# Delta-rule attention with a two-level expert layer: values times norms made two chunks in advance, inverses spread a period behind their last step, selection products a period behind their factors

## The chip, the cores and the metric

The kernel is one program on one core of a Trainium2 chip. The metric is the device time of one launch in microseconds (us). The core's engines each run their own queue in the order in which the program was written: TensorE (PE) multiplies matrices, VectorE (DVE), ScalarE (ACT) and GpSimd (POOL) work elementwise, SyncE (SP) starts most of the transfers. An engine waits at an instruction until the results it needs are there, and everything behind that instruction in the same queue waits with it.

## The reference: what is computed

Two stages, one after the other. The first is a delta-rule attention over 4 batches x 8 heads, 768 steps, head size 48. The second routes each of the 3072 tokens to one of 4 groups, then to one of 4 experts in it, and applies that expert's two matrices.

```python
k_n = k / (norm(k) + 1e-6)
for t in range(S):                         # S = 768
    y[t]  = q[t] @ state
    v_old = k_n[t] @ state
    state = state + beta[t] * outer(k_n[t], v[t] - v_old)
x = y as (3072 tokens, 384)
g = argmax(x @ w_group); e = argmax(x @ w_expert[g])
out = softmax weight of g * softmax weight of e * (relu(x @ w1[g, e]) @ w2[g, e])
```

## The kernel before

**Chunks and periods.** The 768 steps are cut into `NCH` = 24 chunks of `C` = 32 steps; a chunk holds 4 batches x 32 steps = 128 tokens, so it fills the 128 partitions. One pass of the loop `for u in range(NCH + 1)` (line 612) is called a period here. Period u advances chunk u through the recurrence (`advance(u)`), and beside it works ahead and behind for other chunks. All work of the four engines in this part is written out by hand in one order (a `manual_schedule`); no scheduler moves it.

**The recurrence** (`advance`, four steps between its yields). L355 puts the scaled values `vh` into a PSUM tile `a_ps`, L361 adds keys times the old state `s_bd`; ScalarE copies it to `f` (L365); L370 makes the queries' part of the output in `o_ps`. L377 multiplies `f` by the chunk's inverse `mtb` to `w_ps`, ScalarE copies that to `w` (L380). L387 adds keys times `w` to the state in PSUM, ScalarE copies the state to `s_bd` (L393, two instructions). L398 finishes `o_ps`, ScalarE copies it to `x` (L402).

**The inverse.** Inside a chunk the 32 steps depend on each other; `inverse(g)` removes that with a 32 x 32 triangular inverse for each head, batch and chunk. It works on a group g of `RG` = 4 chunks at once, all on VectorE, in some 105 instructions: a transpose (L243), the norms (L250 to L280, the result `norm`), a scaling of `m` and a tile `cs` (L282, L287), elimination steps (L294, L299, L316, L322), a product with `cs` (L324), and a transpose to `mt` (L329). `mt` takes the buffer of `cs`, of which there is one. Then two ScalarE copies (L334) spread `mt` into the two halves of `mtb`. `gram(u)` makes what the inverse starts from, `LEAD` = 9 chunks ahead: L225 on TensorE, a ScalarE copy `gt` (L228) and a VectorE product `gq` (L233), both out of one PSUM tile of the tag "g".

**The routing.** `logits(u)` transposes `x` (L419, `t_ps`, also tag "g"), copies it (L423) and multiplies by the routing weights (L427, `l_ps`; L429 `lg`). `route(r)` takes the logits of 4 chunks (2 at the end), finds group and expert (VectorE, L454 to L482), counts tokens (POOL `acc` L484; TensorE L490 and L491 into `r_ps`, tag "g" again), and makes each token's place in its expert's list (`rk` L496, `place` L498) and its factors `mine` (L518). For each chunk it then makes a one-hot tile `at` on POOL (L523) and multiplies it with `mine` on TensorE (L529). These selection products collect the token lists in `s_sort`.

**Work that is due later.** `inverse` and `route` are generators. `start` puts one in the list `behind`; `work(n)` lets those with budget left run until each has used its share. A generator can yield a label instead of a number: it then stands still until `allow(label)` is called at a fixed point of the period. `SOON` is allowed near the end of a period, `NEXT` near its start, `SORT` and `ACT_STEP` after `w_ps`, `ACT_STEP` and `PE_STEP` also after the last step, `TURN` when a task ends. What is emitted at such a point stands at that place in the engine's queue, whether its input is ready by then or not.

**Buffers that matter here.** The PSUM tag "g" has one buffer, shared by the tiles of `gram`, `t_ps` and `r_ps`; so has tag "s", shared by `a_ps`, `w_ps` and `l_ps`. `vh`, `at`, `mtb` and `m` have two buffers, `mine` three.

**The second stage** walks the 16 experts in order of their load (a fixed list of row counts, `SLOTS`): gather rows (POOL L719), transpose (L729), two matrix products (L740, L754), transpose back (L766), scale and scatter (L769, L770).

Of the kernel before, what the change touches and what calls it, by code (L numbers as in the profile page):

```python
# [8 lines left out]
F32 = mybir.dt.float32  # L9
# [6 lines left out]
C = 32  # L16
RG = 4
# [4 lines left out]
ACT_STEP, PE_STEP, SOON, NEXT, TURN = "ScalarE", "TensorE", "end of the period", "next period", "its turn"  # L22
# [40 lines left out]
def deltanet_then_moe(  # L63
# [14 lines left out]
    B, H, S, D = shape  # L78
# [75 lines left out]
    with ExitStack() as first:  # L154
# [49 lines left out]
                pieces.pop(0)()  # L204

        rooted = sm.tile([128, 1], F32, tag="rooted", name="rooted", bufs=1)
        gts, gqs, mts, norm, vhs, xs = {}, {}, {}, {}, {}, {}

        def gram(u, home=None):

# [26 lines left out]
        def inverse(g):  # L237
# [43 lines left out]
            yield  # L281
            nc.vector.tensor_tensor(m, m, r0[:, :, None].to_broadcast([128, C, C]), op=ALU.mult)  # L282
            yield C * C
            while g and g - 1 not in mts:
                yield TURN
            cs = wk.tile([128, C, C], F32, tag="cs", name=f"cs{g}", bufs=1)
            nc.vector.tensor_tensor(cs, cut["below"].rearrange("p (i j) -> p i j", i=C),  # L287
# [37 lines left out]
            yield C * C  # L325
            nc.vector.tensor_scalar(diag, r0, -1.0, None, op0=ALU.mult)
            yield
            mt = wk.tile([128, RG * H, C], F32, tag="cs", name=f"mt{g}", bufs=1)
            nc.vector.transpose(out=mt.rearrange("p r i -> p i r"), in_=flat)  # L329
            mtb = wk.tile([128, RG * H, 2, C], F32, tag="mtb", name=f"mtb{g}")  # L330
            yield 2 * C * C
            for a in range(2):
                yield ACT_STEP
                nc.scalar.activation(mtb[:, :, a], mt, ACT.Copy,  # L334
                                     scale=cut["parity"][:, a:a + 1])
            mts[g] = mtb

        def scale(u):

            g, uu = divmod(u, RG)  # L340
            vh = wk.tile([128, H, D], F32, tag="vh", name=f"vh{u}")
            nc.vector.tensor_tensor(  # L342
                vh.rearrange("p (j f) d -> p f j d", f=2),
                kv_[u % NV][:, H * 64:].rearrange("p (j f d) -> p f j d", j=NP, f=2),
                norm[g][:, uu * H:(uu + 1) * H].rearrange("p (f j) -> p f j", f=2)[:, :, :, None]
                .to_broadcast([128, 2, NP, D]), op=ALU.mult)
            vhs[u] = vh
# [84 lines left out]
        def route(r):  # L432
# [53 lines left out]
            if n == RG:  # L486
# [31 lines left out]
            nc.vector.tensor_tensor(mine, hotf[:, :, None, :].to_broadcast(like),  # L518
                                    what[:, u0:u0 + n, :, None].to_broadcast(like), op=ALU.mult)
            yield 128  # L520
            for g, u in enumerate(us):
                at = wk.tile([128, T, TILE], F32, tag="at", name=f"at{u}")
                (nc.gpsimd if n == RG else nc.vector).tensor_scalar(  # L523
                    at.rearrange("p t i -> p (t i)"), cut["places"], place[:, u:u + 1], None,
                    op0=ALU.is_equal)

                yield SORT
                for t in range(T):
                    nc.tensor.matmul(s_sort[:, t * 3 * NE:(t + 1) * 3 * NE], lhsT=at[:, t],  # L529
                                     rhs=mine[:, g].rearrange("p c e -> p (c e)"),  # L530
                                     start=False, stop=True, skip_group_check=True)
# [19 lines left out]
        def work(n):  # L551


            for task in behind:
                due[task] = min(due[task] + n * 180 * rate[task], 4000.0)
            while True:
                able = [t for t in behind if held.get(t) is None and due[t] > 0]
                if not able:
                    break
                for task in able:  # L560
                    push(task)

        def allow(what):

            for task in list(behind):
                if held.get(task) is what:
                    push(task)
# [5 lines left out]
        with tc.manual_schedule(engines={mybir.EngineType.PE, mybir.EngineType.DVE,  # L573
                                         mybir.EngineType.Activation, mybir.EngineType.Pool}):
            nc.scalar.activation(rooted, cut["tiny"], ACT.Exp)
            homes = [None, s_ps[:, 0:2], s_ps[:, 2:4]]
            masks = []
            for u in range(RG):
                if u == len(homes):
                    masks.pop(0)()  # L580
                masks.append(gram(u, homes[u % len(homes)]))
                if u == 1:

                    nc.scalar.activation(kqt_[RG][:, 0, 0, 0:1], cut["tiny"], ACT.Copy)
                    load_rest()
            start(inverse(0), 1)
            for step in range(RG):
                work(6)
                masks.pop(0)()
                work(6)  # L590
                allow(ACT_STEP)
                allow(SOON)
                allow(NEXT)
                masks.append(gram(RG + step, homes[(RG + step) % len(homes)]))
            while behind:
                work(4)
                allow(ACT_STEP)
                allow(SOON)
                allow(NEXT)
                if masks:  # L600
                    masks.pop(0)()
            scale(0)
            nc.gpsimd.memset(acc[:, 0], 0.0)
            nc.gpsimd.tensor_copy(what[:, :, 0:2], cut["ids"].rearrange("p (u c) -> p u c", c=2))
            start(inverse(1), SHARE)
            for step in range(4):
                work(14)
                allow(ACT_STEP)
                allow(SOON)
                allow(NEXT)  # L610
                if step < LEAD - 2 * RG:
                    gram(2 * RG + step)()
            for u in range(NCH + 1):
                step = advance(u) if u < NCH else iter([None] * 4)
                turned = logits(u - 1) if u else iter([None] * 2)
                next(step)
                allow(NEXT)
                r = group_of.get(u - 2)
                if r is not None and group_of.get(u - 1) != r and r < NGR - 2:
                    start(route(r), 0.25)  # L620
                next(turned)
                if u + 1 < NCH:
                    scale(u + 1)
                work(16)
                next(step)
                allow(SORT)
                allow(ACT_STEP)
                masks = gram(u + LEAD) if u + LEAD < NCH else lambda: None
                work(9)
                masks()  # L630
                work(8)
                next(step)
                next(turned)
                next(step)
                allow(PE_STEP)
                allow(ACT_STEP)
                r = group_of.get(u - 1)
                if r is not None and group_of.get(u) != r and r >= NGR - 2:
                    start(route(r), 0.6 if r == NGR - 2 else 1)
                allow(SOON)  # L640
                if u % RG == RG - 2 and u // RG + 2 < NGR:
                    start(inverse(u // RG + 2), SHARE)
                work(12)
                if u + NB < NCH:
                    load_kq(u + NB)
                if u + NV < NCH:
                    load_kv(u + NV)
                if u < NCH:
                    nc.sync.dma_start(out=x_dram[u * 128:(u + 1) * 128], in_=xs[u])
                if pieces and u >= RG:  # L650
                    pieces.pop(0)()
            while behind:
                work(2)
                allow(PE_STEP)
                allow(ACT_STEP)
                allow(SOON)
                allow(NEXT)
                allow(SORT)

            n_ps = ps.tile([128, NE], F32, tag="s", name="n_ps")  # L660
            nc.tensor.matmul(n_ps, lhsT=ones, rhs=acc[:, NCH], start=True, stop=True)
            nc.vector.tensor_copy(found.rearrange("p t c e -> p (t c e)"), s_sort)
            by_place(found[:, :, :, 0:FIXED], slice(0, FIXED))
            nc.vector.tensor_copy(last, n_ps)


            key, rank = cp.tile([128, NE], F32, name="key"), cp.tile([128, NE], F32, name="rank")
            nc.vector.scalar_tensor_tensor(key, in0=last, scalar=16.0, in1=cut["tie"], op0=ALU.mult,
                                           op1=ALU.add)
            like = [128, NE, NE]  # L670
            nc.vector.tensor_tensor(table, key[:, None, :].to_broadcast(like),
                                    key[:, :, None].to_broadcast(like), op=ALU.is_gt)
            nc.vector.tensor_reduce(rank, table, axis=AX.X, op=ALU.add)
            nc.vector.tensor_tensor(table, rank[:, None, :].to_broadcast(like),
                                    cut["expert"][:, :, None].to_broadcast(like), op=ALU.is_equal)
# [241 lines left out]
```

## Time and profile before

Three launches took 583.02, 583.09 and 580.49 us, median 583.02. The profiled launch took 582.09 us, of which the profile shows a span of 580.3 us.

| engine | busy us | share of the span |
|---|---|---|
| TensorE matmuls | 502.1 | 87% |
| TensorE weight loads | 459.6 | 79% |
| VectorE | 251.8 | 43% |
| ScalarE | 164.4 | 28% |
| GpSimd | 105.0 | 18% |

The shares are averages over two stages with different limits: from about 288 us on the expert matrices keep TensorE busy without a break, and before that four engines hand work to each other. In the first stage the start of L355 marks the start of a period; the timeline of TensorE has it at these times.

| chunk u | L355 starts at, us | chunk u | L355 starts at, us | chunk u | L355 starts at, us |
|---|---|---|---|---|---|
| 0 | 49.42 | 8 | 130.29 | 16 | 207.31 |
| 1 | 61.85 | 9 | 139.39 | 17 | 216.37 |
| 2 | 71.98 | 10 | 147.77 | 18 | 224.04 |
| 3 | 82.66 | 11 | 157.49 | 19 | 231.71 |
| 4 | 92.66 | 12 | 168.97 | 20 | 239.39 |
| 5 | 100.54 | 13 | 179.11 | 21 | 247.06 |
| 6 | 108.50 | 14 | 187.49 | 22 | 254.89 |
| 7 | 116.79 | 15 | 196.04 | 23 | 262.78 |

Reading a line of the timeline: start in us, length in us, engine, line of the kernel, operation, output <- inputs, shape, number of instructions merged; in brackets how long the engine had been idle before it, and what it waited for. A line of the waits reads: who waited <- for whom: us in total, how often, the longest.

### The profile page before, as it was taken

The numbers are of one execution on the slowest core, as the hardware profiler recorded it, in microseconds if no ns is written. First come the engines' busy times: TensorE is split into PE (matmuls) and PEld (weight loads), VectorE is DVE, ScalarE is ACT, GpSimd is POOL, SyncE is SP. The second block draws the span as 40 slices with busy tenths as digits, with TensorE's granted clock in tenths as the row PEclk, the third lists the DMA queues.
The fourth block names the chain that finished last, engine by engine and source line by source line (L and its number), as shares of the span: only waits on it lengthen the run. The fifth ranks groups of instructions, "written<-read, shape, count | busy, mean of one in ns | idle before, by whom it ended". The sixth has DMA issues, their size and how long they took to land.

```text
span 580.3 us, 18417 instructions
## 1 busy us (share of the span) xinstructions
PE 502.1 (87%) x8166; PEld 459.6 (79%) x8166; DVE 251.8 (43%) x913; ACT 164.4 (28%) x324; POOL 105.0 (18%) x110
## 2 busy tenths in 40 slices
PE   3315779979989899997599999999999999999993
PEld 2214567867767778786599999999999999999993
DVE  1889989898898896123531111110111111111110
ACT  2103345544635545543011111111111111111110
POOL 0000000020021110130234221423225312221111
PEclk9999979989979979998599999999999999999998
DMA  8990334434422222210145747575766775676400
GB/s 280 404 382 12 112 104 152 144 110 136 129 85 81 62 82 89 73 56 31 49 142 155 223 158 224 177 228 178 239 202 192 236 226 204 241 239 216 160 20 18
DMA packets 44322, 90.64 MB, mean 156 GB/s; under 512 B 9756, under 2 KB 29651, under 8 KB 44241
## 3 DMA queue, kind: packets, MB, share of 16 engines
q1 hardware_dynamic: 34256, 79.71, 40.9%
q0 software_dynamic: 9984, 9.74, 6.3%
q8 instruction: 65, 1.06, 0.8%
q14 instruction: 17, 0.13, 0.1%
HBM read 79.92 MB, written 9.66 MB: 154 GB/s over the span
## 4 chain that ended last, share of the span: by engine, by line
issue 32%; PE 21%; DVE 19%; POOL 12%; DMA 9%; ACT 5%; POOLq 0%; SPq 0%; ACTq 0%; DVEq 0%
DMA out_dram<-yo,to_i 8%; POOL xg L719 7%; POOL out_dram L770 5%; DVE m L322 3%; DVE t L316 3%; PE s_ps L387 3%; PE w_ps L377 3%; PE a_ps L355 3%; ACT s_bd L393 3%; PE a_ps L361 2%; DVE m L299 2%; PE s_ps L529 2%; PE o_ps L370 2%; PE l_ps L427 1%; PE t_ps L419 1%
## 5 line engine op out<-in xcount | busy, mean ns | idle before, releaser
L740 PE MATMUL h_ps<-xt,w 128*128 128x224 f32 (+14 forms) x768 | 140.2, 336 | 0.6 <-DVE xt L731 0.6
L754 PE MATMUL y_ps<-hid,w 128*128 128x224 f32 (+14 forms) x768 | 138.8, 334 | 0.0
L740 PEld LDWEIGHTS h_ps<-xt,w 128*128 128x128 f32 x768 | 131.1, 192 | 1.6 <-DVE xt L731 0.9
L754 PEld LDWEIGHTS y_ps<-hid,w 128*128 128x128 f32 x768 | 129.3, 190 | 0.3
L731 DVE COPY xt<-t_ps 128x336 f32<-128x336 f32 (+14 forms) x32 | 15.1, 472 | 141.0 <-PE t_ps L729 141.0
L743 ACT ACTIVATE hid<-h_ps 128x448 f32<-128x448 f32 (+14 forms) x64 | 32.4, 506 | 125.7 <-PE h_ps L740 125.7
L769 DVE TENSOR_SCALAR yo<-o_ps,gate 112x384 f32<-112x384 f32 (+14 forms) x32 | 19.6, 616 | 106.3 <-PE o_ps L766 106.3
L719 POOL DMA_INDIRECT xg<-x_dram,from_i x32 | 39.3, 1227 | 121.5 <-PE t_ps L729 100.1
L770 POOL DMA_INDIRECT out_dram<-yo,to_i x32 | 39.2, 1226 | 101.8 <-DVE yo L769 100.9
L316 DVE TENSOR_TENSOR t<-m 128x81 f32<-128x81 f32 (+13 forms) x156 | 51.3, 329 | 0.2
L322 DVE TENSOR_TENSOR m<-m,t 128x81 f32<-128x81 f32 (+13 forms) x156 | 50.6, 324 | 0.0
L756 ACT ACTIVATE yt<-y_ps 128x224 f32<-128x224 f32 (+14 forms) x48 | 16.2, 338 | 120.2 <-PE y_ps L754 120.2
L355 PE MATMUL a_ps<-vh,con 128*128 128x384 f32 x48 | 26.2, 633 | 26.0 <-DVE vh L342 15.2
L393 ACT ACTIVATE s_bd<-s_ps 48x768 f32<-48x768 f32 x46 | 37.1, 806 | 22.2 <-PE s_ps L387 21.7
L299 DVE SCALAR_TENSOR_TENSOR m<-m 128x29 f32<-128x29 f32 (+27 forms) x174 | 39.2, 228 | 0.4
L523 POOL TENSOR_SCALAR at<-con,place 128x256 f32<-128x256 f32 x20 | 20.8, 1047 | 97.4 <-PE s_ps L529 49.7
L355 PEld LDWEIGHTS a_ps<-vh,con 128*128 128x128 f32 x48 | 8.4, 219 | 28.7 <-DVE vh L342 15.4
L377 PEld LDWEIGHTS w_ps<-f,mtb 64*64 64x64 f32 x768 | 25.3, 138 | 7.0 <-issue 4.9
L377 PE MATMUL w_ps<-f,mtb 64*64 64x48 f32 x768 | 28.5, 224 | 1.7 <-ACT f L365 1.0
L361 PEld LDWEIGHTS a_ps<-s_bd,kqt 128*32 128x32 f32 x736 | 17.0, 120 | 15.2 <-issue 15.2
L387 PE MATMUL s_ps<-w,kv 32*128 32x96 f32 x736 | 28.8, 296 | 0.2
L484 POOL TENSOR_TENSOR acc<-acc,hots 128x16 f32<-128x16 f32 x20 | 5.1, 256 | 129.2 <-DVE hots L482 128.0
(117 smaller groups left out, 551.6 us busy)
## 6 DMA issues: line engine op xcount, KB each, us to landing
w<-in_w_dram SPq DMA_DIRECT2D x28, 1536.0 KB, 7.5
kqt<-in_kq_dram SPq DMA_DIRECT2D x24, 512.0 KB, 5.1
kv<-in_kv_dram SPq DMA_DIRECT2D x24, 448.0 KB, 3.4
x_dram<-x SPq DMA_DIRECT2D x24, 192.0 KB, 2.3
w<-in_w_dram SPq DMA_DIRECT2D x6, 512.0 KB, 9.7
w<-in_w_dram SPq DMA_DIRECT2D x4, 576.0 KB, 10.1
w<-in_w_dram SPq DMA_DIRECT2D x2, 384.0 KB, 9.6
con<-in_const_dram SPq DMA_DIRECT2D x1, 512.0 KB, 8.2
```

Of the source, the lines that this page charges most:

```text
L299: nc.vector.scalar_tensor_tensor(row, in0=m[:, j, 0:j], scalar=m[:, i, j:j + 1], in1=row, op0=ALU.mult, op1=ALU.add)
L316: nc.vector.tensor_tensor(tv, m[:, j + 2:, j:j + 1].to_broadcast([128, n, j]), m[:, j:j + 1, 0:j].to_broadcast([128, n, j]), op=ALU.mult)
L322: nc.vector.tensor_tensor(below, below, tv, op=ALU.add)
L355: nc.tensor.matmul(a_ps.rearrange("p h d -> p (h d)"), lhsT=ident, rhs=vh.rearrange("p h d -> p (h d)"), start=True, stop=(u == 0), skip_g ...
L377: nc.tensor.matmul(w_ps[b, h], lhsT=mt[b, uu * H + (h % 2) * NP + h // 2], rhs=f[b, h], start=True, stop=True, skip_group_check=True)
L387: nc.tensor.matmul(s_at[:, b, j], lhsT=k[quads[b], j], rhs=w[quads[b], 2 * j:2 * j + 2], start=(u == 0 and j == 0), stop=True, skip_group_ ...
L393: nc.scalar.activation(s_bd[rows, :, :, hh, :], s_at[rows, :, :, hh * D:(hh + 1) * D], ACT.Copy)
L719: nc.gpsimd.indirect_dma_start(out=xg[0:P, t, :], out_offset=None, in_=x_dram[:, :], in_offset=bass.IndirectOffsetOnAxis(ap=rows[0:P, t:t ...
L740: nc.tensor.matmul(h_ps[:, k], lhsT=w1[:, j, (f + k) * 128:(f + k + 1) * 128], rhs=xt[:, j], start=(j == 0), stop=(j == DC - 1), skip_grou ...
L743: nc.scalar.activation(hid[:, f:f + 2], h_ps, ACT.Relu)
L754: nc.tensor.matmul(y_ps, lhsT=w2[:, f, j * 128:(j + 1) * 128], rhs=hid[:, f], start=(f == 0), stop=(f == FC - 1))
L770: put = nc.gpsimd.indirect_dma_start(out=out[:, :], out_offset=bass.IndirectOffsetOnAxis(ap=to[0:P, i:i + 1], axis=0), in_=yo[:, :], in_of ...
```

## The change

The order of three kinds of work is moved; no arithmetic is added or removed.

1. `scale(u)`, the product of values and norms `vh`, is made two chunks ahead instead of one: the first two before the loop, and `scale(u + 2)` near the end of period u in place of `scale(u + 1)` in its middle.
2. After the transpose L329 the inverse of every group but the first waits for the start of the next period before it spreads `mt` over `mtb` on ScalarE. Since `mt` then lives longer, it gets a buffer of its own, and the next group's `cs` waits for the transpose (`turned_over`) instead of for `mtb`; `TURN` is allowed once in every period.
3. In `route`, for the groups of four chunks, the one-hot tiles `at` and with them the selection products L529 wait for the end of the period after `mine`, so the first product stands a period later in TensorE's queue.

The purpose is that the engine which uses a result finds it ready when its turn comes.

```diff
-        gts, gqs, mts, norm, vhs, xs = {}, {}, {}, {}, {}, {}
+        gts, gqs, mts, norm, vhs, xs, turned_over = {}, {}, {}, {}, {}, {}, set()
...
-            while g and g - 1 not in mts:
+            while g and g - 1 not in turned_over:
                 yield TURN
             cs = wk.tile([128, C, C], F32, tag="cs", name=f"cs{g}", bufs=1)
...
-            mt = wk.tile([128, RG * H, C], F32, tag="cs", name=f"mt{g}", bufs=1)
+            mt = wk.tile([128, RG * H, C], F32, tag="mt", name=f"mt{g}", bufs=1)
             nc.vector.transpose(out=mt.rearrange("p r i -> p i r"), in_=flat)
             mtb = wk.tile([128, RG * H, 2, C], F32, tag="mtb", name=f"mtb{g}")
             yield 2 * C * C
+            turned_over.add(g)
+            if g:
+                yield NEXT
             for a in range(2):
                 yield ACT_STEP
...
             yield 128
+            if n == RG:
+                yield SOON
             for g, u in enumerate(us):
                 at = wk.tile([128, T, TILE], F32, tag="at", name=f"at{u}")
...
             scale(0)
+            scale(1)
...
                 next(step)
                 allow(NEXT)
+                allow(TURN)
...
                 next(turned)
-                if u + 1 < NCH:
-                    scale(u + 1)
                 work(16)
...
                 work(12)
+                if u + 2 < NCH:
+                    scale(u + 2)
                 if u + NB < NCH:
```

## The prediction

> **What bounds the kernel now.** I read the page's slices first (40 of 14.5 us; tenths of busy time).
>
> ```profile
> PE   3315779979989899997599999999999999999993
> DVE  1889989898898896123531111110111111111110
> PEclk9999979989979979998599999999999999999998
> ```
>
> From slice 20 (290 us) on, TensorE is full at the full clock and VectorE nearly idle: the second stage lasts as long as its matmuls, and only its start can move. In slices 3 to 15 TensorE has holes, VectorE is nearly full, and the clock dips in four places. So the first stage decides, and there I read the waits from 75 to 285 us.
>
> ```profile
> PE s_ps L529 <- DVE mine L518: 7.1, 3, 3.0
> ACT mtb L334 <- DVE mt L329: 3.2, 2, 2.7
> PE t_ps L419 <- DVE rk L496: 0.6, 2, 0.4
> ```
>
> Small sums, but the table of L355 starts shows their weight: an undisturbed period is 8.38 us (chunk 9 to 10), 7.88 without L529 (4 to 5), 7.68 without gram (17 to 18). Period 7 lasted 13.50, 11 11.48, 15 11.27, each with one of the L529 waits. TensorE's timeline from 119 to 128 us shows the wait, and a second loss behind it:
>
> ```profile
> 119.84 1.13 PE L377 MATMUL w_ps<-f,mtb 64*64 64x48 f32 x32
> 123.96 0.62 PE L529 MATMUL s_ps<-mine,at 128*128 128x48 f32 x4 [2.99 <-DVE mine L518]
> 125.50 2.04 PE L387 MATMUL s_ps<-w,kv 32*128 32x96 f32 x32
> ```
>
> L387 takes 2.04 us where it takes 1.15 in a quiet period (175.94 us): the clock is at half. The clock column puts four such spells in the first stage, at 80.6 to 87.4, 125.0 to 131.8, 165.9 to 172.7 and 203.5 to 210.3, 6.8 us each. From L529 in period 7 to the start of chunk 9 are 15.43 us; undisturbed, (8.38 - 3.84) + 8.38 = 12.92. A spell thus costs about 2.5 us on top of the wait.
>
> The spell at 80.6 has another cause, seen on ScalarE from 76 to 84 us:
>
> ```profile
> 76.10 0.49 ACT L380 ACTIVATE w<-w_ps 128x384 f32<-128x384 f32 x1 [0.74 <-PE w_ps L377]
> 79.30 1.15 ACT L334 ACTIVATE mtb<-mt,con 128x1024 f32<-128x1024 f32 x1 [2.71 <-DVE mt L329]
> 80.36 0.58 ACT L228 ACTIVATE gt<-g_ps 128x256 f32<-128x256 f32 x1
> 80.74 1.66 ACT L393 ACTIVATE s_bd<-s_ps 48x768 f32<-48x768 f32 x2
> ```
>
> ScalarE stands at `mtb` until the transpose is done, with `gt` and the state copy `s_bd` ready behind it (L387 began at 76.78), and chunk 3 starts at 82.66 instead of 71.98 + 7.96 = 79.94.
>
> **The Trainium skill.** "TensorE: Matmul & The Clock Gate", Part 1 (The HAM clock gate), says the clock halves after an idle window of about 3.4 us and comes back after a busy one. The trace agrees in length (6.8 us is two windows) but not in the trigger: the 1.66 us wait at 163.64 sufficed. The same page, under "Architectural detail", says ScalarE and VectorE queues are strictly first in, first out; the stop at 79.30 agrees. Every other price below is this trace's.
>
> **The change, part by part.**
>
> *1, `vh` two ahead.* Between the old and new places almost nothing is emitted for VectorE, so its queue keeps its order with two exceptions. First, `vh` 1 moves from behind 40 inverse instructions to directly behind `vh` 0. Before, L355 of chunk 1 waited for it; the timelines of PE and DVE:
>
> ```profile
> 57.07 1.50 PE L398 MATMUL o_ps<-w,gq 32*32 32x48 f32 x64
> 61.85 1.62 PE L355 MATMUL a_ps<-vh,con 128*128 128x384 f32 x2 [3.27 <-DVE m L299]
> 66.12 0.90 PE L419 MATMUL t_ps<-con,x 128*128 128x128 f32 x3
> ```
>
> ```profile
> 61.16 0.55 DVE L342 TENSOR_TENSOR vh<-kv,normt 128x384 f32<-128x384 f32 x1
> 65.42 0.42 DVE L233 TENSOR_TENSOR gq<-g_ps,con 128x256 f32<-128x256 f32 x1
> ```
>
> L355 can start at 58.6. But L419 behind it needs the tag "g" tile that `gq` reads until 65.84, and as many instructions precede that `gq` as before. The 3.3 us become a wait at L419. Between nothing gained and a cold spell lost (2.5) I take 0. Second, `vh` 8, 12, 16, 20 go ahead of `rk` instead of behind: `rk` is 0.54 us later, and L419, queued behind it through tag "g", with `w_ps` and all of TensorE behind that. I count this below. The values' transfer lands in 3.4 us (median) and is issued a period earlier, so it adds no wait.
>
> *2, `mtb` a period later.* Same two copies of 1.15 us. The 2.71 us stop and its spell go (period 3: 10.00 against 7.88, so 2.1): 4.8 us. New cost: in periods 3 and 7 the first copy plus `gt` (1.15 + 0.63) stands behind `w`, where the state copy comes 1.46 us after `w`: 0.3 each. Where L529 also lies there, it is hidden (153.09: `s_bd` still on time). The second copy falls just ahead of `f`, before which ScalarE idles 1.4 us. Also `gt` of periods 6, 10, 14 no longer stands behind a copy, so VectorE waits less for it.
>
> *3, L529 a period later.* Removes three waits (7.1 us) and three spells (2.5 each): 14.6 us at most. `at` on POOL (0.95 us) and `mine` are then ready about a period early. At the end one product more falls after chunk 22; it is 0.5 us, of which part lies beside the last routing: I take 0.3.
>
> Parts 2 and 3 offer 4.8 + 14.6 = 19.4 us. VectorE decides how much is kept. From one L243 to the next:
>
> ```profile
> 115.46:155.13 39.67, 33.68 (x134) 0.91 0.38 122
> ```
>
> ```profile
> DVE gq L233 <- ACT gt L228: 12.3, 8, 2.8
> ```
>
> Of those 39.67 us it waited 0.3 + 2.6 + 2.3 (three of the eight waits for `gt`), so its own pace is 34.5 us for four periods; TensorE's would be 3 x 8.38 + 8.6 = 33.7 (the last with the count L490). VectorE becomes the bound, and I follow it:
> - `vh` 3 ends at 79.68 as before; `gq` no longer waits; L243 of group 2 at 80.1 (81.34 before). Work to the next L243: 34.1 - 1.4 of waits = 32.7, so 112.8. TensorE: chunk 3 at 80.0, 4 at 88.2, 6 at 104.0; then L490 needs the `gq` just ahead of that L243, so chunk 7 starts at 113.6 (before 116.79).
> - `rk` at 112.8 + 3.71 + 0.54 = 117.1; L419 was due at 113.6 + 2.3 = 115.9 and waits till 117.3. From L419 to the next L355 is 5.6 + 0.3: chunk 8 at 123.2, 9 at 131.6, 10 at 140.0, 11 at 148.6 (157.49).
> - L243 at 147.3, `rk` 151.6, L419 waits 0.7: chunk 12 at 157.8, 15 at 183.2; L243 181.8, `rk` 186.1: chunk 16 at 191.6 (207.31).
> - From L243 to the end of `vh` 19 is 33.2 us of work: 215.0, and chunk 19 starts at 215.1 (231.71): 16.6 earlier. Then nothing changes but 0.2 in period 22 and the 0.3 at the end: **16.5 us**.
>
> Each new wait at L419 (1.5, 0.7, 0.7) can bring a spell, 2.5 us. Where VectorE is the bound a spell early on is mostly absorbed, since the next L419 then finds `rk` done; the last is not. I subtract one: **14.0 us, 569.0**.
>
> **Rivals.**
> - No spell: 583.0 - 16.5 = 566.5. For it: waits of 0.7 are shorter than the 1.66 that caused one. Against: the 1.5 in period 7.
> - A wait takes the place of the one removed in full: the three `rk` waits each bring a spell and none is absorbed: 16.5 - 7.5 = 9.0, 574.0. For it: before, all three short waits on L529 brought one. Against: VectorE idles 12.3 us in 80 to 228, which a slow TensorE uses up first.
> - No change: TensorE gains in the chunks and loses it at the gather or the weights. Against: the profile shows no wait for weights in the second stage. 583.
> - Slower: the deferred copies meet a late transpose directly ahead of `f` and stop ScalarE there, 4.8 us in each of five groups: 583 + 24 - 16.5 = 590.5. Against: by the times above L329 ends 112.0 and its copy is due at about 121.8.
>
> **How the numbers follow.** One spell left 0.47, none 0.25, three 0.20, no change 0.04, slower 0.04. The likeliest gives 569.0. The range leaves out the last two and allows about 2 us beyond the outer cases, for the unknown of part 1 and the start of the second stage: 564.5 to 575.5. All of the first three are more than 0.5% (2.9 us) faster: 0.92, 0.04, 0.04.
>
> **What the profile after would show.** Right: no wait of L529 for `mine`; `mtb` never waits for `mt`; chunk 7 near 113.6, 11 near 148.6, 19 near 215; VectorE's wait for `gt` down from 12.3 us to below 3; new waits of L419 for `rk` or `gq` (chunk 1: about 3 us). Wrong: clock dips in periods 11 and 15 as before; L355 waiting for `vh` in the middle of a group; `at` or `mine` still late for L529; or a second stage longer than the 292 us from 288.19 to the end.

## The result and the profile after

Four launches of the changed kernel had a median of 568.14 us (566.69 to 569.3), four of the kernel before, on the same chip, 583.06 us. The ratio is 0.9747, interval [0.9702, 0.9791]: 14.9 us less. The span went from 580.3 to 567.1 us. The three rows of the page's slices that were read before, now 14.2 us to a slice:

```profile
PE   3314799999999999996799999999999999999993
DVE  1889989999998994225501111111011111111110
PEclk9999779999989999995699999999999999999998
```

TensorE's row (slices counted from 0) is at 9 from 5 to 17 without a break, VectorE's at 8 or 9 from 1 to 14. Of the four dips of the clock in the first stage two are left: one in slices 4 and 5, earlier than any before, and a small one in slice 11. The dip at the turn to the second stage (18 and 19 here, 19 and 20 before) is in both. The waits from 75 to 272 us (who waited <- for whom: us in total, times, longest):

```profile
DVE gq L233 <- ACT gt L228: 4.5, 3, 2.2
...
PE t_ps L422 <- DVE rk L499: 2.3, 3, 1.2
```

Before, VectorE waited 12.3 us for `gt` within 80 to 228. The selection product (now L534) no longer appears waiting for `mine`, nor `mtb` for `mt`. In their place stand the three waits for `rk`, 2.3 us in all.

What was lost is on TensorE's timeline in two places. In period 1:

```profile
58.16 1.65 PE L358 MATMUL a_ps<-vh,con 128*128 128x384 f32 x2
...
65.09 0.90 PE L422 MATMUL t_ps<-con,x 128*128 128x128 f32 x3 [3.28 <-DVE gq L233]
...
68.91 2.04 PE L390 MATMUL s_ps<-w,kv 32*128 32x96 f32 x32
```

and in period 11:

```profile
152.57 0.55 PE L422 MATMUL t_ps<-con,x 128*128 128x128 f32 x3 [0.78 <-DVE rk L499]
...
157.60 0.35 PE L390 MATMUL s_ps<-w,kv 32*128 32x96 f32 x2 [0.51 <-issue]
...
159.94 1.65 PE L358 MATMUL a_ps<-vh,con 128*128 128x384 f32 x2 [0.41 <-ACT lg L432]
```

The 3.27 us that L355 waited in period 1 before have become 3.28 at L422, and L390 behind it takes 2.04 us, not 1.15: half clock, in the records from 64.3 to 78.0 us. In period 11 three small gaps (0.78, 0.51, 0.41) precede a start of chunk 12 at half clock (1.65 for 0.86), from 159.9 to 163.3. "Issue" in a bracket is a gap in which TensorE waited for nothing the profile shows.

| start of chunk | before | forecast | after |
|---|---|---|---|
| 3 | 82.66 | 80.0 | 83.51 |
| 7 | 116.79 | 113.6 | 114.77 |
| 8 | 130.29 | 123.2 | 123.79 |
| 11 | 157.49 | 148.6 | 149.47 |
| 12 | 168.97 | 157.8 | 159.94 |
| 15 | 196.04 | 183.2 | 186.66 |
| 19 | 231.71 | 215.1 | 217.56 |
| 23 | 262.78 | - | 248.23 |

Chunk 22 of the kernel before starts at 254.74 us, not at 254.89 as in the first table.

### The profile page after: what moved, and what is told of

The parts are those of the page before. It is cut to its first block, busy times and chain, and to the rows that moved or that the text cites. A ratio compares the mean times of both kernels' runs of the same rounds, so it can differ in the third digit from the quotient of the medians.

```text
span 567.1 us, 18415 instructions
## 1 busy us (share of the span) xinstructions
PE 498.2 (88%) x8166; PEld 456.9 (81%) x8166; DVE 250.7 (44%) x913; ACT 164.4 (29%) x324; POOL 105.8 (19%) x110
## 3 DMA queue, kind: packets, MB, share of 16 engines
q8 instruction: 65, 1.06, 0.8%
## 4 chain that ended last, share of the span: by engine, by line
issue 33%; DVE 21%; PE 20%; POOL 12%; DMA 9%; ACT 3%; POOLq 0%; SPq 0%; ACTq 0%; DVEq 0%
DMA out_dram<-yo,to_i 8%; POOL xg L726 7%; POOL out_dram L777 5%; DVE t L316 4%; DVE m L322 4%; PE w_ps L380 3%; PE s_ps L390 3%; DVE m L299 3%; ACT s_bd L396 3%; PE s_ps L534 2%; PE a_ps L358 2%; PE a_ps L364 2%; PE o_ps L373 2%; PE t_ps L422 2%; PE g_ps L225 1%
## 5 line engine op out<-in xcount | busy, mean ns | idle before, releaser
L358 PE MATMUL a_ps<-vh,con 128*128 128x384 f32 x48 | 24.8, 601 | 21.2 <-DVE vh L345 15.2
L299 DVE SCALAR_TENSOR_TENSOR m<-m 128x29 f32<-128x29 f32 (+27 forms) x174 | 39.6, 230 | 0.4
L390 PE MATMUL s_ps<-w,kv 32*128 32x96 f32 x736 | 28.5, 292 | 0.6 <-issue 0.5
L358 PEld LDWEIGHTS a_ps<-vh,con 128*128 128x128 f32 x48 | 8.0, 208 | 23.9 <-DVE vh L345 15.4
```

Of the source, the lines that this page charges most:

```text
L299: nc.vector.scalar_tensor_tensor(row, in0=m[:, j, 0:j], scalar=m[:, i, j:j + 1], in1=row, op0=ALU.mult, op1=ALU.add)
L358: nc.tensor.matmul(a_ps.rearrange("p h d -> p (h d)"), lhsT=ident, rhs=vh.rearrange("p h d -> p (h d)"), start=True, stop=(u == 0), skip_g ...
L390: nc.tensor.matmul(s_at[:, b, j], lhsT=k[quads[b], j], rhs=w[quads[b], 2 * j:2 * j + 2], start=(u == 0 and j == 0), stop=True, skip_group_ ...
```

## The experiments

Each run was timed beside the kernel before on the same chip; ratios are to that.

**Each part alone.** The edits are the numbered parts of the change, each applied to the kernel before.

```diff
# part 1
             scale(0)
+            scale(1)
...
-                if u + 1 < NCH:
-                    scale(u + 1)
...
+                if u + 2 < NCH:
+                    scale(u + 2)
```

> Only the values made two chunks ahead (part 1). Theory V (VectorE's pace is the bound once parts 2 and 3 are in, and part 1 changes its queue only at two spots): no gain, 583 to 585 us; L355 of chunk 1 starts near 58.5 us, L419 behind it waits about 3.3 us for gq, a slow-clock spell follows in period 1, and from chunk 3 on (82.7 to 83.5) all is as before. Rival A (the three parts' gains simply add): part 1 gives the 3.3 us of the wait for vh, 579.8. Rival B (the values two ahead are what gives the gain): 570 or less.

582.7 us, ratio 1.0022 [1.0005, 1.004]: slightly slower. TensorE in period 1:

```profile
57.31 1.65 PE L355 MATMUL a_ps<-vh,con 128*128 128x384 f32 x2
...
64.23 0.90 PE L419 MATMUL t_ps<-con,x 128*128 128x128 f32 x3 [3.19 <-DVE gq L233]
```

The same move of the wait from L355 to L419, and half clock from 63.6 to 77.3 us. Chunk 3 starts at 82.70, as before. So part 1 brings its own spell, and nothing else was gained.

```diff
# part 2
-            while g and g - 1 not in mts:
+            while g and g - 1 not in turned_over:
...
-            mt = wk.tile([128, RG * H, C], F32, tag="cs", name=f"mt{g}", bufs=1)
+            mt = wk.tile([128, RG * H, C], F32, tag="mt", name=f"mt{g}", bufs=1)
...
+            turned_over.add(g)
+            if g:
+                yield NEXT
...
+                allow(TURN)
```

> Only the inverses spread a period later (part 2). Theory V: chunk 3 starts at about 80 instead of 82.7, chunk 7 at about 113.5 (VectorE lets no more through), and the waits of L529 for mine come back after it, a little shorter since gt no longer stands behind a copy: 3.3 to 6 us faster, about 578. Rival A: 4.8 - 0.6 = 4.2 faster, 578.8, with the waits of L529 as long as before. Rival B: nothing but the 2.7 us stop, 580.3.

579.74 us, 0.9964 [0.9938, 0.999]. The waits of TensorE from 75 to 285 us begin with

```profile
PE s_ps L532 <- DVE mine L521: 7.0, 3, 2.6
```

so the waits for `mine` stay. Chunk 3 starts at 79.56 (3.1 earlier) and chunk 7 at 113.1 (3.7), but chunk 23 only 2.3 earlier: the early gain is partly given back where `mine` is late.

```diff
# part 3
             yield 128
+            if n == RG:
+                yield SOON
```

> Only the selection products a period later (part 3). Theory V: the three waits of L529 go, chunk 8 near 125 (130.3 before), but as TensorE comes forward ScalarE stops at mtb for mt in periods 10, 14 and 18 too, longest in 18 (about 4 us, with a spell): 9 to 11 us faster, about 573. Rival A: the waits and their spells, 14.6 us, 568.5. Rival B: the waits come back at rk, 580 or more.

572.65 us, 0.9839 [0.982, 0.9857]. No wait for `mine` is left; ScalarE's waits from 44 to 275 us have instead

```profile
ACT mtb L334 <- DVE mt L329: 29.7, 6, 17.6
```

and its timeline two of the stops:

```profile
111.81 1.15 ACT L334 ACTIVATE mtb<-mt,con 128x1024 f32<-128x1024 f32 x1 [1.25 <-DVE mt L329]
147.31 1.15 ACT L334 ACTIVATE mtb<-mt,con 128x1024 f32<-128x1024 f32 x1 [2.48 <-DVE mt L329]
```

Besides the 17.6 us at the start, which every version has, that is five stops and 12.1 us, where the kernel before had two and 3.2 us. TensorE is now earlier, VectorE is not, so the transposes come late for ScalarE; period 18, 7.67 us before, takes 10.65.

**Parts 2 and 3 together**, without part 1:

> Parts 2 and 3 without the values two chunks ahead. Theory V: no wait of L419 for gq and no spell in period 1, chunk 3 at about 80, rk half a microsecond earlier in each group; VectorE's pace then gives 1 to 2 us less than the changed kernel: about 566.5. Rival A: part 1's 3.3 us are missing, 571.5. Rival B: hardly faster than before, 580.

566.18 us, 0.9709 [0.9677, 0.9742]: 15.65 us less. Alone, the two saved 2.1 and 9.2. They are not additive: each wait removed lets another come forward, here ScalarE's for `mt`, which part 2 removes. Chunk 7 starts at 113.89 and 19 at 216.45.

This run also corrects the reading of the spell at 80.6 us. TensorE ahead of it, first in the kernel before, then here:

```profile
79.59 0.29 PE L427 MATMUL l_ps<-wr,xt 128*128 128x20 f32 x1 [1.01 <-issue]
...
82.66 1.65 PE L355 MATMUL a_ps<-vh,con 128*128 128x384 f32 x2 [1.97 <-ACT lg L429]
```

```profile
80.03 0.29 PE L430 MATMUL l_ps<-wr,xt 128*128 128x20 f32 x1 [1.01 <-issue]
...
81.40 1.65 PE L358 MATMUL a_ps<-vh,con 128*128 128x384 f32 x2
```

The spell began at 80.6, ahead of the 1.97 us that the stop at `mtb` cost L355. What precedes it in both kernels is the same gap of 1.01 us ahead of the same matmul. With the stop gone the spell still comes, at 80.6 to 84.0: 3.4 us of it instead of 6.8. Part 2 alone has it too, at 78.6 to 82.0.

**Only `vh` 1 put back.** The changed kernel, with `vh` 1 again in the middle of period 0; `vh` 8, 12, 16 and 20 stay ahead of `rk`.

```diff
-            scale(1)
...
+                if u == 0:
+                    scale(1)
                 work(16)
```

> The changed kernel with the product vh of chunk 1 put back behind the inverse's first instructions; all later vh stay two chunks ahead. Theory V: the spell of period 1 in the changed kernel came from this product alone (L358 starts early, L422 then idles 3.3 us), so no spell there, chunk 2 at about 72 and chunk 3 at about 81 instead of 73.7 and 83.5; VectorE's pace absorbs most of it: 566 to 568 us. Rival A: 3.3 us lost at L358 and nothing else, 571.5.

566.03 us, 0.9708 [0.9677, 0.9739]. TensorE in period 1:

```profile
60.78 1.62 PE L358 MATMUL a_ps<-vh,con 128*128 128x384 f32 x2 [3.27 <-DVE m L299]
...
64.82 0.55 PE L422 MATMUL t_ps<-con,x 128*128 128x128 f32 x3 [0.22 <-DVE gq L233]
...
70.51 0.91 PE L358 MATMUL a_ps<-vh,con 128*128 128x384 f32 x2
```

The wait is back at the head of the period, and there is no spell there: chunk 2 starts at 70.51 where the changed kernel has 73.71, chunk 7 at 112.83 for 114.77. The order of instructions decides when the 3.3 us fall. In the kernel before and here, they end at 61.9 and 60.8, while TensorE is still at the half clock with which it began the stage (it rises at 66.9 and 63.9). With part 1 whole, the work ahead of the wait brings the clock up at 60.9, and the wait, 61.8 to 65.1, takes it down again. The ratio equals that of parts 2 and 3, which fits a cost of part 1 that lies in this one instruction. Its size is not settled: the ratio is 2.2 us below the changed kernel's 0.9747, but the intervals overlap, and in the profiled launches chunk 23 starts only 0.4 us earlier (247.82 for 248.23), since this version has two later spells (139.0 and 159.5) where the changed kernel has one.

**More work for VectorE.** `vh` is computed a second time, into a tile that nobody reads, in 16 periods of the kernel before and of the changed one. A product takes 0.48 us from start to start: 7.7 us.

```diff
+                if 3 <= u < 19:
+                    twice(u + 1)
                 work(16)
```

> The kernel before with 16 more VectorE instructions, one in each of periods 3 to 18: the product vh of the next chunk once more into a spare tile (0.48 us each, 7.7 us in all). Theory V: VectorE idles 12.3 us there and takes most of it up, only mine and mt come half a microsecond later: 1.5 to 3.5 us slower than before, about 584.5. Rival C (TensorE with its clock, not VectorE, sets the pace in both kernels): within 1.5 us of before.

> The changed kernel with the same 16 added VectorE instructions (7.7 us in all). Theory V: VectorE idles only 4.5 us there, so 4 to 7.7 us come through, 572 to 576 us, with L422 waiting longer for rk and gq. Rival C: within 1.5 us of the changed kernel, 568 to 569.5.

Before: 585.98 us, 1.0068 [1.0046, 1.0089], 3.9 us more, more than expected; VectorE's waits for `gt` in 80 to 228 fell from 12.3 to 8.9, and TensorE's for `mine` stayed about the same (6.9 for 7.1). After: 573.94 us, 0.9845 [0.9802, 0.9888]; against the changed kernel's 0.9747 that is 0.0098 x 582 = 5.7 us more. The longer waits at the transpose (now L433) that were expected did not come: there TensorE waits 1.8 us for `rk` (2.3 in the changed kernel) and, in period 1, 4.1 for `gq` (3.3; 4.0 in a second trace of the changed kernel). New are two other waits:

```profile
114.56 0.43 PE L504 MATMUL r_ps<-hots,con 128*128 128x64 f32 x2 [1.13 <-DVE gq L233]
...
223.15 1.62 PE L369 MATMUL a_ps<-vh,con 128*128 128x384 f32 x2 [1.32 <-DVE vh L345]
```

New too are a spell of 10.2 us from 120.4 and one of 3.4 from 222.8. From L243 of group 3 to that of group 4 VectorE takes 36.92 us, 0.7 of it waits, where the changed kernel takes 34.29. Work added to VectorE was paid at half its price before and at three quarters after; at the start of chunk 23 the traces are 3.7 and 7.0 us behind, of 7.7. Little slack is left.

**Less work for VectorE, by moving it.** From chunk 2 on, the changed kernel's `vh` on GpSimd.

```diff
-            nc.vector.tensor_tensor(
+            (nc.gpsimd if u > 1 else nc.vector).tensor_tensor(
```

> The changed kernel with the products vh from chunk 2 on made by GpSimd instead of VectorE: takes about 0.5 us a chunk from VectorE, 8 us by chunk 19. Theory V: four periods of VectorE fall from 34.5 to about 32.5 us, TensorE's 33.7 to 34 become the bound, rk is no longer late for L422, the spell of period 12 goes: 3 to 5 us faster than the changed kernel, about 564. Rival C: nothing gained, 568. Rival D (GpSimd's slow product, perhaps 1.5 to 2 us, holds up the one-hot tiles or slows VectorE beside it): slower than the changed kernel, 570 or more.

570.49 us, 0.979 [0.9761, 0.9818]: no gain, and 2.5 us above the changed kernel by these ratios. From one `gq` to another VectorE took 8.35 us (124.37 to 132.72) without `vh`, and 8.23 (124.26 to 132.49) with it in the changed kernel; from L243 of group 3 to that of group 4 it took 34.97 us for 34.29, with one wait of 0.22 in between. VectorE's timeline in the kernel before, then here, then GpSimd's here:

```profile
147.86 0.69 DVE L299 SCALAR_TENSOR_TENSOR m<-m 128x29 f32<-128x29 f32 x3
...
149.85 0.20 DVE L326 TENSOR_SCALAR m<-r 128x32 f32<-128x32 f32 x1
```

```profile
143.12 1.47 DVE L299 SCALAR_TENSOR_TENSOR m<-m 128x29 f32<-128x29 f32 x3
144.63 1.23 DVE L324 TENSOR_TENSOR m<-m,cs 128x1024 f32<-128x1024 f32 x1
145.89 0.71 DVE L326 TENSOR_SCALAR m<-r 128x32 f32<-128x32 f32 x1
```

```profile
143.27 0.83 POOL L345 TENSOR_TENSOR vh<-kv,normt 128x384 f32<-128x384 f32 x1
...
144.97 1.57 POOL L345 TENSOR_TENSOR vh<-kv,normt 128x384 f32<-128x384 f32 x1
```

L299 is longer here by 0.78 us, about the one product of 0.83 that lies beside it. The second product starts under L324, takes 1.57, and ends at 146.54, and L326, which had taken 0.20, takes 0.71 and ends at 146.60. It looks as if one waits for the other. The Trainium skill, "SBUF — State Buffer", Who interferes with whom, says that a VectorE instruction with two SBUF inputs or in a two-port mode and a GpSimd instruction that reads SBUF exclude each other for a whole instruction. These durations agree.

**An earlier `rk`.** On parts 2 and 3, the inverse gets a smaller budget in the period ahead of `rk`, and what it lost there a period later; nothing is left out.

```diff
-                work(16)
+                work(21 if u % RG == RG - 1 else 16)
...
-                if u % RG == RG - 2 and u // RG + 2 < NGR:
+                fresh = u % RG == RG - 2 and u // RG + 2 < NGR
+                if fresh:
                     start(inverse(u // RG + 2), SHARE)
-                work(12)
+                work(7 if fresh else 12)
```

> Parts 2 and 3, and the share of the inverse that is emitted ahead of rk cut from ten instructions to two (work(7) instead of work(12) in the period that starts an inverse, work(21) instead of work(16) in the next), so rk stands some 2.5 us earlier in VectorE's queue and nothing is left out. Theory V: the waits of L422 for rk in periods 7, 11 and 15 go, and the spell near 155 to 162 us with them; VectorE's pace is unchanged: 1 to 3 us faster than parts 2 and 3, 564. Rival E (the spell comes from other gaps, or gq then comes too late): no difference, 566.

566.17 us, 0.9718 [0.9689, 0.9748]: no gain. Counted from L243, `rk` of groups 3 and 4 stands 2.0 and 1.3 us earlier than in parts 2 and 3, somewhat less than planned. L422's waits for `rk`, 1.1 us in parts 2 and 3 (0.8 on this chip), are down to 0.4, and L358 waits another 0.4 for it, but the spell at 155 us stayed. The wait for `rk` is not its cause, or not alone.

**Less work for VectorE, left out.** On parts 2 and 3, the tile `cs` of groups 2 to 5 is not computed; that of group 1 is used, so the result is not the inverse.

```diff
+            if g < 2:
+                kept["cs"] = wk.tile([128, C, C], F32, tag="cs", name=f"cs{g}", bufs=1)
+                nc.vector.tensor_tensor(kept["cs"], ...)
+            cs = kept["cs"]
```

> Parts 2 and 3 with one VectorE instruction of 1.1 to 1.4 us left out in each of the four groups from 2 on: L287, so these groups use the tile cs of group 1 and their result is not the inverse. Theory V: VectorE's 34.5 us for four periods fall to about 33.2, below TensorE's 33.7 to 34; 3 to 4.5 us faster than parts 2 and 3, about 562.5. Rival C (TensorE sets the pace): no difference, 566.

565.74 us, 0.9713 [0.9683, 0.9742]: no gain from some 5 us less, as the rival expected. VectorE's waits from 80 to 228 us:

```profile
DVE gq L233 <- ACT gt L228: 5.2, 4, 2.7
DVE rk L503 <- PE r_ps L498: 1.1, 1, 1.1
```

6.3 us, where parts 2 and 3 on the same chip have 3.3. About 3 of the 5 us that VectorE no longer works it waits, and TensorE's undisturbed periods stay at 8.38 and 7.68.

**Once more, on one chip.** The changed kernel and parts 2 and 3, beside the last two:

> The changed kernel once more, beside the others on one chip: 568 us; ratio to the kernel before 0.975.

> Parts 2 and 3 without part 1, once more beside the changed kernel. Theory V: 1 to 2 us below the changed kernel (no spell in period 1), 566.3; a rival that holds part 1 for a gain expects 569 or more.

566.77 us, 0.9723 [0.9693, 0.9752], and 564.53 us, 0.9692 [0.9659, 0.9724]. By these ratios parts 2 and 3 without part 1 were about 2 us below the changed kernel both times (0.9709 against 0.9747, 0.9692 against 0.9723). The intervals overlap each time; here, on one chip, the launches were 562.29 to 566.71 and 565.67 to 567.43 us. The traces give about half of it to the first stage: chunk 23 starts 1.1 us earlier the first time (247.12 for 248.23) and 1.0 the second (245.27 for 246.26). The rest of the second difference arose after it, where the spell at the turn lasted 23.9 us in the changed kernel and 17.1 in parts 2 and 3, though it lasted 23.9 in both the first time. How much of that is part 1's is not shown. Even two traces of the changed kernel differ by 2.0 us at chunk 19 (217.56 and 215.60). Parts 2 and 3 are the fastest version run.

## Why the prediction was right

The forecast was 569.0 us, the measurement 568.14. Parts 2 and 3 worked for the stated reasons; that the sum came so close is in part luck. It subtracted one spell, 2.5 us, and chunk 19 starts at 217.56, 2.5 after the 215.1 that was forecast without one. But the spells behind this difference, and their causes, are not those of the forecast, and in a second trace of the same kernel chunk 19 starts at 215.60.

- **Part 3's waits and part 2's stops go: right.** Neither appears in the profile after. The gains of 14.6 and 4.8 us offered were indeed not kept in full, though part 3 alone kept 9.2 and part 2 alone 2.1, and the two together 15.65.
- **VectorE's pace: right.** It was forecast at 34.5 us for four periods. In the profile after, L243 of group 4 follows that of group 3 by 34.29 us, with no wait of VectorE between. Its waits for `gt` from 80 to 228 us were forecast below 3 us; 4.5 were left.

```profile
113.91 1.22 DVE L243 STREAM_TRANSPOSE m<-gt 128x1024 f32<-128x1024 f32 x1
...
148.20 1.22 DVE L243 STREAM_TRANSPOSE m<-gt 128x1024 f32<-128x1024 f32 x1
```

- **VectorE becomes the bound: half right.** Its margin to TensorE's forecast 33.7 us is 0.8 in four periods. The runs show a balance: in the changed kernel added work is mostly paid, but in parts 2 and 3 5 us less gave nothing. The expectations that rested on VectorE alone, for the product on GpSimd, for `rk` and for `cs`, failed.
- **Part 1 at nothing: the step that failed.** "Between nothing gained and a cold spell lost (2.5) I take 0." It was the lost spell, and a long one, 13.7 us at half clock (10.2 in the second trace). Period 1 took 15.55 us where `vh` 1 put back gives 9.73, and chunk 3 started at 83.51, not 80.0. Of these 3.5 us 1.2 are left at chunk 7 (114.77 for 113.6), where VectorE's pace decides again, and at the end about 1 to 2 us, by the comparisons above. The forecast's argument that an early spell is mostly absorbed fits this, but for a spell it had not entered.
- **One spell left over: right in number, wrong in place and cause.** It was to follow a wait for `rk`, with the last one not absorbed. The waits were smaller than forecast (2.3 us for 1.5 + 0.7 + 0.7), and the spell came at the turn from period 11 to 12, 3.4 us long; chunk 12 came 2.1 us late (159.94). With `rk` early it still came.
- **The spell at 80.6 us: wrongly attributed.** "The 2.71 us stop and its spell go", said the prediction. Only the stop went. Parts 2 and 3 keep the spell at half its length, behind a gap of 1.01 us in which TensorE waited for no other engine. In the changed kernel there is none, with the long spell of period 1 ahead of it.
- **The end: sign right, size too small.** The product that falls after chunk 22 was priced at 0.3 us. Chunk 23 is 14.55 us earlier, the first expert product 13.49 (274.70 for 288.19): 1.1 lost in between. The timelines show where. Two products more than before fall after the start of chunk 23: one in period 23 (L534 there takes 1.09 us, L529 before 0.65), and one in the last batch, shown below before and after. That batch lies in the spell at the turn, so its four more matmuls cost 0.85 us, where the four in period 23 cost 0.44. The second stage took 292.4 us against 292.1. (The profiled launch, with its span 13.2 us shorter, is 0.8 us above the median.)

```profile
278.77 1.94 PE L529 MATMUL s_ps<-mine,at 128*128 128x48 f32 x8 [0.21 <-DVE at L523]
```

```profile
264.34 2.79 PE L534 MATMUL s_ps<-mine,at 128*128 128x48 f32 x12 [0.29 <-POOL at L528]
```

- **The rivals.** Without any spell 566.5 was forecast. The versions without the spell in period 1 came to 566.03 and 566.18, but they have spells elsewhere, so this agreement is chance. Three unabsorbed spells, no change and slower did not occur: ScalarE has no stop at `mtb` after the first.

## What to carry to other kernels

Before an edit that removes a wait, follow the freed engine to the next shared buffer in its queue: if that buffer is held by the same late instruction, the wait only moves, and it can move to where it costs the clock. When two engines are within some 2% of each other, as here, price an edit on either from both sides: added work can be paid where removed work is not. Test the parts of a change alone and together; here the best version leaves one part out.

## What the runs showed of the hardware

**Gaps at fixed matmul counts: TensorE's own instructions come late.** The 1.01 us ahead of the sixth L427 lies at matmul 1239 of the program, counted from 0, in the kernel before and in parts 2 and 3. Other gaps within a group of equal matmuls lie at the numbers 2640, 2894, 3149, 3276, 3403, 3531 and 3658, or one later, in steps of 127 and 128 or twice that. They last 0.2 to 1.3 us, each is found in several versions, and the numbers are the same whatever is computed beside. The page of the changed kernel lists a transfer queue (packets, MB, share of 16 engines)

```profile
q8 instruction: 65, 1.06, 0.8%
```

65 packets of 16 kB for 8166 matmuls and as many weight loads are one packet for 126 matmuls. The traces hold the times of these packets. The same number of matmul goes with the same packet in all fourteen traces, 1239 with the ninth, 3658 with the 28th. At thirteen such places (those above and 984, 1112, 1366, 1493 and 2257) there are 70 gaps of 0.15 us or more, and each ends 1.23 to 1.59 us after its packet has landed. At the other 112 passes TensorE goes on 1.21 to 6.45 us after it, never sooner. So TensorE waits there for its instructions; no run moved the packets to try it.

The gap at 3658 (0.51 to 1.06 us, in the state product of period 11) stands ahead of the spell of periods 11 and 12 in the changed kernel, in parts 2 and 3, with `rk` early and with `cs` left out.

**What brings the clock down.** Spells in the first stage last a multiple of 3.4 us: 3.4, 6.8, 10.2, 13.7. TensorE's busy time in the window of that length ahead of a spell, in the kernel before (start:end length, busy us and count, clock, share and rate of transfers):

```profile
121.60:125.00 3.40, 1.04 (x52) 0.99 0.10 39
162.50:165.90 3.40, 2.26 (x100) 1.00 0.03 11
```

The first is 31% busy, the second 66%. The Trainium skill, "TensorE: Matmul & The Clock Gate", Part 1, asks for an idle window. Here, once the clock had first risen, every full-clock window of the first stage up to 45% busy was followed by a spell, in all fourteen traces. Of those of 50 to 80% some were, and some were not (66% at 115.5 us of the changed kernel had none). The share does not decide alone: a spell follows a window of 87% in part 3 alone (74.1 to 77.5 us), and the spell at the turn one of 91% in the changed kernel (252.07 to 255.48 us). What decides stays open.
